# Key sums of a linear-attention layer with the exponentials as weights and the values moving, and variance from centred squares, in a four-layer kernel

## The chip, the cores and the metric

The kernel runs on one core of a Trainium2 chip. The metric is the device time of one execution in microseconds, lower is better; a kernel's time is the median of several runs. The core has a matrix engine (TensorE, PE in the profile, with its weight loads in a row of their own, PEld), a vector engine (VectorE, DVE), a scalar engine for functions and copies (ScalarE, ACT), GpSimd (POOL) and a queue that issues transfers (SyncE, SP). Each engine works through its own list of instructions in order and waits on semaphores for the others. Matmuls write to PSUM, eight banks of 512 float32 values in each of 128 partitions; the operands of matmuls lie in SBUF.

## The reference

Two kinds of layer alternate, A, B, A, B, each on a normalised input and added to it. There are 2048 tokens, 512 features, 32 heads of 16.

```python
def _A_ref(x, wqkv, w_phi, wo):
    B, S, D = x.shape
    H = 32; Dh = D // H
    qkv = (lambda x, *d: x.transpose(*d))((x @ wqkv).reshape(B, S, 3, H, Dh), 2, 0, 3, 1, 4)
    q, k, v = qkv[0], qkv[1], qkv[2]
    pq = jnp.einsum("bhsd,hdf->bhsf", q, w_phi)
    pk = jnp.einsum("bhsd,hdf->bhsf", k, w_phi)
    phi_q = jnp.concatenate([_softmax(pq, axis=-1), _softmax(-pq, axis=-1)], axis=-1)
    phi_k = jnp.concatenate([_softmax(pk, axis=-1), _softmax(-pk, axis=-1)], axis=-1)
    kv = jnp.einsum("bhsf,bhsd->bhfd", phi_k, v)
    z  = jnp.einsum("bhsf->bhf", phi_k)
    num = jnp.einsum("bhqf,bhfd->bhqd", phi_q, kv)
    den = jnp.einsum("bhqf,bhf->bhq", phi_q, z)[..., None] + 1e-6
    o = num / den
    return (lambda x, *d: x.transpose(*d))(o, 0, 2, 1, 3).reshape(B, S, D) @ wo
...
x = x + _A_ref(_layernorm(x, axis=-1), A_wqkv, A_w_phi, A_wo)
x = x + _B_ref(_layernorm(x, axis=-1), B_wqkv, B_wo)
x = x + _A_ref(_layernorm(x, axis=-1), A_wqkv, A_w_phi, A_wo)
x = x + _B_ref(_layernorm(x, axis=-1), B_wqkv, B_wo)
```

Layer A is linear attention: `kv` and `z` sum over all tokens, once per head, before any query can be answered. These are the key sums. Layer B is attention over eight earlier tokens at a distance of two, with the same weights in both of its layers.

## The kernel before

The 2048 tokens are 16 tiles of 128, held as four blocks b of four tiles; `x` stays in SBUF in bf16. Weights stay in SBUF too; at the start, w_phi is multiplied into the query and key columns of layer A's weights (`s_fold`), so that a projection gives `pq` and `pk` directly. L is 0 or 1, the first or second pair of layers.

Layer A runs in these steps. `s_a1`, per block: for each tile `mk` projects the keys (four matmuls, line 632), `ek` takes the exponentials of plus and minus the result (line 638, the index s is the sign), `mv` projects the values (line 644) and `ev` copies them into the tile `va`; VectorE adds up the 16 exponentials of each head and sign, ScalarE forms the inverse (`rr`), and VectorE multiplies it in (`mul`, line 690). `kv` (lines 697 to 709) then adds the tile to the key sums in PSUM. `va` holds 16 groups of 32 value columns (two heads) and a column of ones each. The 33 columns of a group are the weights of a matmul and 2 x 32 columns of exponentials move, so a tile takes 16 matmuls; two groups lie side by side in the halves of the array (`tile_position`). One bank holds all sums, with values on partitions and exponentials on columns. A matmul by zeros (line 700) prepares it.

`s_a2` projects the queries (line 737), takes their exponentials Eq (line 745) and their sums per head, S (line 753). `s_akv`, once per layer, turns the key sums into what the queries need: the bank is copied to `kvT`, four transposes put the exponentials on partitions (line 783), `z` writes the sums of ones, masked by head, into ZM (line 792), and `r` writes the value sums, masked by `mask2`, into R (line 796).

`s_a3`, per block: the denominator from ZM and Eq (line 821); `dr`, `ln` and `rho` go from VectorE to ScalarE and back to VectorE (lines 829 to 840); rho is spread over the features by matmuls (line 847, from where it goes to the products on line 855, in some cases through a copy `bs`) or, for two blocks of each layer, through a transfer. `s_a4`: the product of Eq and R (line 940), copied to `oT`, and the output projection in `s_out` (line 553).

`s_out` ends all layers. `res` adds the old x to the projection and sums each row (`sums`), on VectorE (line 571), or on ScalarE (line 568) after a matmul by the identity on PE (line 556). `sq` has ScalarE square the row and sum it (line 578). `var` (lines 588 and 590, VectorE) takes the squared mean off, and `s_norm` forms the inverse deviation (lines 450 and 453), the shift (line 457) and the normalised tile xn (line 466 or 468), which is transposed by PE (line 482) or by a transfer.

Layer B has its projections (line 967), elementwise products with eight shifted key windows (line 1059), sums per head by a matmul (line 1066), softmax, products with shifted values (line 1121), sums (line 1128) and `s_out`. The last block but the end of the second B layer goes another way, by small matmuls (lines 1185 to 1380).

What sets the order: each step is put into a thread named after its stage and engine, and `_ORDER` is a list of thread numbers in base 36; the program takes the next step of the thread that each number names. So it fixes every engine's list. `_CHOICE` has a digit for each step that either engine can do, 1 for VectorE (and, in `res`, for the identity matmul on PE with ScalarE), 0 for ScalarE, as `flex` and `copy` show; in `res` a 1 stands for the matmul. `_SLOTS` names the buffer or PSUM bank of each tile in turn. At the end a flag decides whether a general version is run instead (lines 1568 on); with these inputs it is not.

Of the kernel before, what the change touches and what calls it, by code (L numbers as in the profile page):

```python
# [16 lines left out]
P = 128  # L17
# [16 lines left out]
VCH = NB * 8 * DV  # L34
EST = (1, 3)
# [25 lines left out]
8 2 i 2e 3s e3 ce 2p 23 i a 5l i i 9 i i i 5o i i i i 4e e7 1m i 0 3u 3r 0 f i e c j b 2 k 3 4 j o 5q 1m l 3 m  # L61
p 1n 0 i 1 n 1t e4 o 1o q 1m 1p r 0 1m 1u s 1m z 5k z z 5 1m 1r 7 6 z 20 20 7 1q 1s 1t 21 21 t 20 20 1v 22 10
z 22 1t 7 1t 20 1w 22 t 11 24 24 13 u 12 16 12 1t t 15 1t v 12 12 22 x 18 14 1x d w w 1y 2c y 18 18 26 18 2d
1f 2d 2c 1z 2d 24 2d 27 17 19 18 1a 1b 21 1c 1d 22 21 22 39 1e 20 20 22 39 25 2c 3b 3a 3a 1f 3a 2d 3a 2f 2c 1f
1f 39 ch 22 2f 2d 2g 1g 29 1f 2d 1j 2f 2d 7 1h 29 1i 1k 3a 29 2n 29 2i 2n 3c 2o 2o 2o 2k 2o 2k 2q 1l cd 2h 2n
2a 2k 2f 2n 2k 3a 2o 2j 24 2q 2r 2q 2o 2o 2o 29 2y 28 2y 2y 3c 2l 2z 2v 2z 2s 2z 2z 2k 2y 2z 39 36 31 2z 36 2z
3a 3b 36 36 2v 31 2v 37 2v 31 2t 36 2z 36 2b 2b 2b 2b 2m 2m ci 36 36 2m 3a 2w 2m 2v 33 34 32 31 3c 35 2q 3c 36
3b 2x g 2x 2u 2x 30 37 2x 36 38 38 38 38 3i 3c 3h 3c 39 3b 3a 3j 3k 3k 3k 3c 3d 3c 3e 3l 3b 3m 3d 3e 5h 3n 3m
3c 3e 3e 3l 5i 3m 3q 3m 3m 4f 3m 3d 3l 5j 3e 3e 3m 5i 3m 3m 3v 3d 3e 3e bd 5h 5m 5n 5i 5i 5i 3m 3d 3e 7c 5h 7d
5p 5i 5i 5i 5r 3f 3g 3g 5i 3f 3g 5i 3w 3f 3z 3x 3f 3g 5s 3y 7e 40 41 3g 7d 5u 5v 7f 5t 3g 3p 41 42 41 41 44 3g  # L70
43 3g 43 5w 5x 5x 7f 45 46 43 43 47 43 7f 5y 3f 90 47 48 49 3g 4c 91 5x 41 4b 41 41 41 4a 92 5x 4d 60 91 4l 5z
61 5z 93 5z 4q 62 5z 4g 7d 4g 4g 4m 4q 63 ck 5z 7d 4r 93 4i 4l 63 66 64 67 7g 4s 7j 65 7h 7i 4h 4j 7k bo 4n 4q
4q 4u 4w 91 7l 4t 7l 7l 7m 7l 7o 68 7n 7n 4l 7p 3h 7n 7q 4w 93 4v 7n 4v 3o 91 4f 6a 7r 4o 6b 7n 6k 6f 69 4g 4k
4l 7r 6l 7s h 4w 6g 6k 6m 4p 6a 6c 6p 7t 7u 6a 6k 6f 6n 7v 4w 6k 6h 94 6r 6d 4x 4x b2 6r 4x 97 6o 98 4x 95 6f
69 7x 96 99 99 9a 4y 6i 99 7w 9b 6q 9c 6q 9d 9b 9b 99 9e 9b 6r 6a 6e 6f 6j 83 84 d4 6q 7y 9f 7y 9b 6r 6s 6s 6s
6s 9f 9h 9i 4y 9g 4w 8d 80 9j 7z 6t 6t 3t 88 6s 83 89 6t 88 88 88 8a 8b 8f 8c 7y 6r 7x 4x 9l 6u 9k 6u 4y 6u 4w
6q 6u 83 85 83 86 87 81 9r 9w 7y 9w 9s 9x 4v 82 4v 9w 6v 9y 9z 4z a1 6v 4z 6v 6w 4z 8e 6v 4z 6y 9m 6x 6z 70 9n
70 70 71 72 73 70 9m 74 72 72 8e 9m 50 50 50 75 50 9o 72 51 9r 52 76 53 8f 54 55 72 9p 9w 76 8f 79 55 77 7a 9r
9t 55 58 78 7b 9u 55 9r 56 9m 8f 59 8g 57 5a 57 8e 8g a3 8g 8g 57 bz b0 8e 9q 57 9v a0 5b 57 8h a3 5b bz 8h a3
8g 5d c0 5e 5c 5f c0 c0 b0 c0 bz 8h b1 5g b3 b1 8f b0 b1 b3 a2 b1 a4 c0 b1 a4 b1 a3 a4 a2 a4 b4 b5 a5 bz a5 8i  # L80
8i c0 8i a2 b3 a4 a2 c0 bx b6 c0 b3 a5 by bx by by b0 b7 bx by by by a3 8i bx 8j 8j b1 8j 8l a6 8k 8j 8m b1 8n
ap by aq aq ap a6 aq aq 8o 8o 8p by 8r 8o 8o 8q 8s 8q as 8t 8q as ap 8q au as ap a6 8u 8q a7 aq at 8u 8w aq bz
# [2043 lines left out]
```

## Time and profile before

| | |
|---|---|
| runs shown | 319.6, 319.8 and 320.18 us, median 319.8 |
| span of the profiled execution | 318.1 us |
| granted TensorE clock | 1.000 |
| instructions | 8900 |
| key sums (line 707) | 512 matmuls, from 44.4 to 203.7 us, in two bursts |
| squares (line 578) | 48 of 0.631 us on ScalarE |
| variance (lines 588 and 590) | 12 and 12 of 0.16 us on VectorE |
| transfers | 36.37 MB, mean 114 GB/s |

The span goes from the first to the last instruction of one execution, taken by the hardware profiler; it is 1.7 us under the median of the runs. Busy time counts an engine's instructions and not its waits; a matmul's row also holds the modelled time until its result is there, so the starts of neighbouring matmuls tell their real distance. The chain of waits is followed back from the last instruction, at each step to what released it or to the instruction before it on its engine.

### The profile page before, as it was taken

To read this page: it belongs to the slowest core of one execution; us is meant where nothing else is said; L and a number is where in the kernel's file an instruction comes from. 1 tells how busy PE (TensorE), PEld (TensorE's weight loads), DVE (VectorE), ACT (ScalarE), POOL (GpSimd) and SP (SyncE) were. 2 spreads that over 40 slices of the span, in tenths; PEclk is the share of its full clock that TensorE was granted. 3 is DMA by queue.
4 is the path that set the end of the run, shared out by engine and by line. 5 is a ranking of instruction groups with operands and counts; after the bars stand their busy time and mean duration, and the time that the engine had idled before them with its cause. 6 is when DMAs were issued, how large, how long until landed. Compare 5 with 4: busy or idle time off the path is not lost.

```text
span 318.1 us, 8900 instructions
## 1 busy us (share of the span) xinstructions
PE 307.7 (97%) x3578; PEld 152.9 (48%) x3578; DVE 295.6 (93%) x459; ACT 275.0 (86%) x639; POOL 47.2 (15%) x60
## 2 busy tenths in 40 slices
PE   8999999899999999999999999989999999999994
PEld 4644456445454444444444455544444544444552
DVE  6999996998999999999999999689998999999994
ACT  4999999999898778999999999899999867697751
POOL 6000000000004212000000000033141644045000
PEclk9999999999999999999999999999999999999999
DMA  7977100005794989939894600004289875565664
GB/s 203 358 186 148 36 2 4 2 19 145 165 178 100 156 141 136 144 66 140 145 134 62 69 0 2 4 19 134 59 185 137 140 133 134 105 178 126 158 152 170
DMA packets 45789, 36.37 MB, mean 114 GB/s; under 512 B 30832, under 2 KB 41136, under 8 KB 45744
## 3 DMA queue, kind: packets, MB, share of 16 engines
q1 hardware_dynamic: 45216, 35.75, 56.3%
q8 instruction: 29, 0.48, 0.7%
q14 instruction: 16, 0.13, 0.2%
q10 hardware_dynamic: 528, 0.02, 0.1%
HBM read 11.13 MB, written 3.25 MB: 45 GB/s over the span
## 4 chain that ended last, share of the span: by engine, by line
PE 87%; DVE 5%; ACT 5%; DMA 1%; issue 1%; SPq 0%; DVEq 0%; ACTq 0%
PE PS L967 23%; PE PS L553 18%; PE PS L632 9%; PE PS L644 9%; PE PS L737 6%; PE PS L1128 4%; PE PS L1066 4%; PE PS L1185 2%; DVE Eq L855 2%; PE PS L707 2%; PE PS L940 1%; PE PS L482 1%; PE PS L556 1%; PE PS L1200 1%; PE PS L1082 1%; DMA x<-in_A_x_dram 1%
## 5 line engine op out<-in xcount | busy, mean ns | idle before, releaser
L967 PE MATMUL PS<-xnT,WB 128*128 128x512 bf16 x336 | 76.8, 380 | 0.1
L1059 DVE TENSOR_TENSOR prod<-QT,K 128x4096 bf16<-128x4096 bf16 x28 | 63.4, 2287 | 0.5 <-POOL K L993 0.5
L1121 DVE TENSOR_TENSOR pav<-PT,Vg 128x4096 bf16<-128x4096 bf16 (+1 forms) x29 | 62.9, 2214 | 0.2
L967 PEld LDWEIGHTS <-WB 128*128 128x128 bf16 x336 | 37.3, 114 | 36.4 <-issue 3.3
L745 ACT ACTIVATE Eq<-PS 128x512 bf16<-128x512 f32 x64 | 36.3, 619 | 0.0
L638 ACT ACTIVATE Ek<-PS 128x512 bf16<-128x512 f32 x64 | 35.1, 622 | 0.2 <-PE PS L632 0.2
L553 PEld LDWEIGHTS <-oT 128*128 128x128 bf16 x236 | 21.9, 98 | 26.6 <-issue 1.3
L737 PE MATMUL PS<-xnT,WA 128*128 128x512 bf16 x128 | 32.0, 380 | 0.5 <-DVE s L829 0.3
L578 ACT ACTIVATE sqd<-x 128x512 bf16<-128x512 bf16 x48 | 29.9, 631 | 2.2 <-DVE x L571 2.0
L644 PE MATMUL PS<-WA,xnT 128*128 128x512 bf16 x128 | 31.6, 379 | 0.0
L632 PE MATMUL PS<-WA,xnT 128*128 128x512 bf16 x128 | 31.0, 379 | 0.2 <-ACT WA L204 0.2
L571 DVE SCALAR_TENSOR_TENSOR x<-PS,x 128x512 bf16<-128x512 f32 x46 | 30.2, 684 | 0.7 <-PE PS L553 0.7
L204 ACT CAST oT<-PS 128x512 bf16<-128x512 f32 (+1 forms) x50 | 26.7, 597 | 3.8 <-PE PS L1128 2.1
L553 PE MATMUL PS<-WoA,oT 128*128 128x512 bf16 x128 | 29.8, 380 | 0.0
L553 PE MATMUL PS<-WoB,oT 128*128 128x512 bf16 x108 | 26.5, 379 | 0.0
L204 ACT CAST K<-PS 128x512 bf16<-128x512 f32 x30 | 17.3, 593 | 3.1 <-PE PS L967 1.9
L632 PEld LDWEIGHTS <-xnT 128*128 128x128 bf16 x128 | 12.3, 98 | 15.2 <-issue 1.0
L644 PEld LDWEIGHTS <-xnT 128*128 128x128 bf16 x128 | 12.2, 98 | 14.5 <-issue 0.4
L690 DVE TENSOR_TENSOR Ek<-Ek,rk 128x4096 bf16<-128x4096 bf16 (+1 forms) x10 | 18.6, 1860 | 0.4 <-ACT rk L685 0.4
L737 PEld LDWEIGHTS <-WA 128*128 128x128 bf16 x128 | 11.6, 98 | 14.6 <-issue 1.7
L466 DVE TENSOR_SCALAR xn<-x,rstd,nmr 128x512 bf16<-128x512 bf16 x48 | 18.1, 424 | 0.6
L204 ACT CAST V<-PS 128x512 bf16<-128x512 f32 x26 | 15.2, 596 | 2.6 <-PE PS L967 2.6
(175 smaller groups left out, 505.1 us busy)
## 6 DMA issues: line engine op xcount, KB each, us to landing
Vg<-V SPq DMA_DIRECT2D x112, 131.5 KB, 4.3
Prho<-rd SPq DMA_DIRECT2D x8, 512.0 KB, 6.1
x<-in_A_x_dram SPq DMA_DIRECT2D x3, 512.0 KB, 6.6
WB<-in_B_wqkv_dram SPq DMA_DIRECT2D x3, 512.0 KB, 9.8
out_dram<-x SPq DMA_DIRECT2D x6, 256.0 KB, 2.3
wraw<-in_A_wqkv_dram SPq DMA_DIRECT2D x4, 256.0 KB, 4.5
vd<-Vs SPq DMA_DIRECT2D x2, 272.0 KB, 2.9
x<-in_A_x_dram SPq DMA_DIRECT2D x4, 128.0 KB, 3.4
```

The source lines that it names most:

```text
L204: self.nc.scalar.copy(out=out, in_=in_)
L553: nc.tensor.matmul(y[:], lhsT=lh(t, c), rhs=Wo()[:, c, :], start=(c == 0), stop=(c == NB - 1 and not onpe))
L571: nc.vector.scalar_tensor_tensor(out=xb[:, t, :], in0=T[t][:], scalar=1.0, in1=xb[:, t, :], op0=ALU.mult, op1=ALU.add, **kw)
L578: nc.scalar.activation(out=sqd[:], in_=xb[:, t, :], func=ACT.Square, accum_out=T["ss"][:, t:t + 1])
L632: nc.tensor.matmul(pk[:], lhsT=xnT[:, t, k, :], rhs=self.WA[:, k, D:2 * D], start=(k == 0), stop=(k == NB - 1))
L638: nc.scalar.activation(out=T["E"][:, t, s, :], in_=T["k", t][:], func=ACT.Exp, scale=1.0 - 2.0 * s)
L644: nc.tensor.matmul(pv[:], lhsT=xnT[:, t, k, :], rhs=self.WA[:, k, 2 * D:3 * D], start=(k == 0), stop=(k == NB - 1))
L737: nc.tensor.matmul(pq[:], lhsT=self.WA[:, k, hb * P:(hb + 1) * P], rhs=xnT[:, :, k, :], start=(k == 0), stop=(k == NB - 1))
L745: nc.scalar.activation(out=self.Eq[L, b][s][:, :, hb, :], in_=T[hb][:].rearrange("p (t i) -> p t i", t=4), func=ACT.Exp, scale=1.0 - 2.0 * s)
L967: nc.tensor.matmul(pp[:], lhsT=self.WB[:, k, i * D + c:(i + 1) * D:NB], rhs=xnT[:, :, k, :], start=(k == 0), stop=(k == NB - 1))
L1059: nc.vector.tensor_tensor(out=pr[:], in0=QT[:, c:c + 1, :].to_broadcast([P, NW, TB]), in1=win, op=ALU.mult)
L1121: nc.vector.tensor_tensor(out=pv, in0=PT[:, :, lo:lo + n].unsqueeze(1).to_broadcast([P, NB, 2, n]), in1=vw, op=ALU.mult)
```

## The change

The key sums are formed the other way round. `ek` writes the exponentials as eight groups of four heads, each with both signs side by side, 128 columns; `va` holds eight groups of 64 value columns and one column of ones. Per tile there are eight matmuls with the 128 columns of exponentials as weights and the 65 columns of `va` moving. The result has exponentials on partitions, so there are no transposes; it fills two banks, groups of even number in one and of odd number in the other, four pieces of 65 columns in each. In `s_akv`, four copies of 64 partitions bring the pieces into R, one per bank and sign; ZM is one product of R's ones column and the head mask; the value sums are masked by `mask4` where they lie in R. The zeroing matmul goes.

The square becomes that of the centred row: ScalarE squares sum - 512 x, with the row's sum as a bias of its own for each partition, so the sum of squares is 512 cubed times the variance, and `var` goes. PHI moves from a constant buffer to a slot that is used again.

`_ORDER`, `_CHOICE` and `_SLOTS` are new throughout. Over the whole program the choices have 14 identity matmuls in place of 17 among the full residuals, and VectorE has more of the copies.

```diff
@@ def sq(t) and norm, in s_out
-            nc.scalar.activation(out=sqd[:], in_=xb[:, t, :], func=ACT.Square, accum_out=T["ss"][:, t:t + 1])
+            nc.scalar.activation(out=sqd[:], in_=xb[:, t, :], func=ACT.Square, scale=-float(D),
+                                 bias=T["sums"][:, t:t + 1], accum_out=T["ss"][:, t:t + 1])
...
-        def var(lo, n):
-            if "q" not in T:
-                T["q"] = self.sm([4], "q")
-            u = T["sums"][:, lo:lo + n]
-            nc.vector.scalar_tensor_tensor(out=T["q"][:, lo:lo + n], in0=u, scalar=-1.0 / D, in1=u,
-                                           op0=ALU.mult, op1=ALU.mult)
-            nc.vector.tensor_tensor(out=T["q"][:, lo:lo + n], in0=T["q"][:, lo:lo + n],
-                                    in1=T["ss"][:, lo:lo + n], op=ALU.add)
-
         def norm(lo, n):
-            add(st, "DVE", var, lo, n)
-            V = {"var": lambda: T["q"][:, lo:lo + n], "sum": lambda: T["sums"][:, lo:lo + n]}
-            self.s_norm(st, key, b, V, tuple(range(lo, lo + n)), 1.0 / D, 1.0 / D)
+            V = {"var": lambda: T["ss"][:, lo:lo + n], "sum": lambda: T["sums"][:, lo:lo + n]}
+            self.s_norm(st, key, b, V, tuple(range(lo, lo + n)), 1.0 / D, 1.0 / D ** 3)
@@ s_a1
-                T["E"] = self.big([4, 2, D], "Ek")
-            nc.scalar.activation(out=T["E"][:, t, s, :], in_=T["k", t][:], func=ACT.Exp, scale=1.0 - 2.0 * s)
+                T["E"] = self.big([4, 8, 2, HQ], "Ek")
+            nc.scalar.activation(out=T["E"][:, t, :, s, :], in_=T["k", t][:].rearrange("p (g c) -> p g c", c=HQ),
+                                 func=ACT.Exp, scale=1.0 - 2.0 * s)
...
-                T["va"] = self.med([4, DH, H + 1], "vaug")
+                T["va"] = self.med([4, 8, HQ + 2], "vaug")
...
         def kv(t):
             if L not in self.kvp:
-                self.kvp[L] = self.ps()
-            K = self.kvp[L]
-            if b == 0 and t == 0:
-                nc.tensor.matmul(K[:], lhsT=self.kvT[:, 0:P], rhs=self.kvT[:], start=True, stop=True)
-            for r in range(4):
-                for h2 in range(2):
-                    for c in range(2):
-                        q = (2 * c + h2) * 4 + r
-                        a = K[64 * c:64 * c + H + 1, h2 * 256 + r * H:h2 * 256 + r * H + 1]
-                        out = bass.AP(a.tensor, a.offset, [list(a.ap[0]), [P, 2], [1, H]])
-                        nc.tensor.matmul(out, lhsT=T["va"][:, t, q, :], rhs=T["E"][:, t, :, q * H:(q + 1) * H],
-                                         start=(b == 0 and t == 0 and r == 0 and h2 == 0),
-                                         stop=(b == 3 and t == 3), tile_position=(0, 64 * c), skip_group_check=True)
+                self.kvp[L] = [self.ps() for _ in range(2)]
+            for g in range(8):
+                c = g // 2 * KVC
+                nc.tensor.matmul(self.kvp[L][g % 2][:, c:c + KVC], lhsT=T["E"][:, t, g, :, :],
+                                 rhs=T["va"][:, t, g, 0:KVC], start=(b == 0 and t == 0 and g < 2),
+                                 stop=(b == 3 and t == 3), skip_group_check=True)
@@ s_akv
-        def ev(dve):
-            self.copy(dve, self.kvT[:], self.kvp[L][:])
-
-
-        def tr():
-            T["t"] = pt = self.ps(BF16)
-            for g in range(4):
-                nc.tensor.transpose(pt[:, g * P:(g + 1) * P], self.kvT[:, g * P:(g + 1) * P], self.ident[:])
...
+        def sh(half, s, dve):
+            self.copy(dve, R[HQ * half:HQ * half + HQ, s, :, 0:KVC],
+                      self.kvp[L][half][HQ * s:HQ * s + HQ, 0:NB * KVC].rearrange("p (b c) -> p b c", c=KVC))
+
+        def z():
+            o = zm[:, 0:1]
+            dst = bass.AP(o.tensor, o.offset, [list(o.ap[0]), [NB * H, 2], [H + 8, NB], [1, 8]])
             m = self.maskH[:]
...
+            nc.vector.tensor_tensor(out=dst, in0=R[:, :, :, HQ:KVC].to_broadcast([P, 2, NB, 8]), in1=msk, op=ALU.mult)
 
         def r():
...
+            v = R[:, :, :, 0:HQ].rearrange("p s b (j d) -> p (s b) j d", d=DH)
+            nc.vector.tensor_tensor(out=v, in0=v, op=ALU.mult,
+                                    in1=self.mask4[:].unsqueeze(1).unsqueeze(3).to_broadcast([P, 8, 4, DH]))
...
+        for half in range(2):
+            for s in range(2):
+                self.flex(st, sh, half, s)
+        add(st, "DVE", z)
+        add(st, "DVE", r)
```

How the new order stands on VectorE at the handover of the key sums of the second layer A, before (PS is PSUM, `ZM_123` is ZM of that layer, `s` and Ds lead to rho):

```order
L690 TENSOR_TENSOR Ek<-Ek,rk 128x2048
L1402 TENSOR_TENSOR nb<-okc,sgn 128x2
L792 TENSOR_TENSOR ZM_123<-PS,maskH 128x2x2x8 x2
L796 TENSOR_TENSOR R<-PS,mask_98 128x256
L829 TENSOR_TENSOR s_3461<-PS,rS 128x256
L832 TENSOR_TENSOR Ds<-s_3461 128x128
L1410 TENSOR_TENSOR nok<-PS,thr 128x2
L1411 TENSOR_REDUCE nf<-nok 128x1
L840 TENSOR_TENSOR rho<-rS,Ds 128x256
```

and VectorE in the same place of the changed kernel, from the last product with the inverse sums on:

```order
L684 TENSOR_TENSOR Ek<-Ek,rk 128x2048
L204 CAST R<-PS 64x4x65
L771 TENSOR_TENSOR ZM_122<-R,maskH 128x2x4x8
L807 TENSOR_TENSOR s_3220<-PS,rS 128x256
L810 TENSOR_TENSOR Ds<-s_3220 128x128
L775 TENSOR_TENSOR R<-R,mask_98 128x8x64
L818 TENSOR_TENSOR rho<-rS,Ds 128x256
```

One of the four copies stands directly ahead of ZM, and the masking of R has moved behind the first steps towards rho; the other three copies are a row `CAST R<-PS 64x4x65 x3` on ScalarE, where one copy of `kvT` stood.

ScalarE at the first norm of the second layer B, before (`x_83` is block 0 of x, lnv and rstd give the inverse deviation):

```order
L568 ACTIVATE x_83,sums<-PS 128x512
L578 ACTIVATE sqd,ss<-x_83 128x512 x2
L835 ACTIVATE Ds<-Ds,deneps_t 128x128
L836 ACTIVATE Ds<-Ds 128x128
L204 CAST oT<-PS 128x512 x2
L578 ACTIVATE sqd,ss<-x_84 128x512
L450 ACTIVATE lnv<-q,eps_t 128x4
L453 ACTIVATE rstd<-lnv 128x4
```

and ScalarE at that norm in the changed kernel:

```order
L570 ACTIVATE x_83,sums<-PS 128x512
L580 ACTIVATE sqd,ss<-x_83,sums 128x512
L813 ACTIVATE Ds<-Ds,deneps_t 128x128
L814 ACTIVATE Ds<-Ds 128x128
L206 CAST oT<-PS 128x512 x2
L580 ACTIVATE sqd,ss<-x_83,sums 128x512
L452 ACTIVATE lnv<-ss,eps_t 128x4
L455 ACTIVATE rstd<-lnv 128x4
```

The logarithm now reads `ss` from ScalarE's own square in place of `q` from VectorE, the last square of the block stands right ahead of it, and each square reads `sums`.

153 lines of the change are left out of this document (70 added, 83 removed).

## The prediction

> **What bounds the kernel now.** I read first the page's busy times and the chain of waits, then busy time by stretches, then single groups and the timeline where the change acts.
>
> ```profile
> PE 307.7 (97%) x3578; PEld 152.9 (48%) x3578; DVE 295.6 (93%) x459; ACT 275.0 (86%) x639; POOL 47.2 (15%) x60
> PE 87%; DVE 5%; ACT 5%; DMA 1%; issue 1%; SPq 0%; DVEq 0%; ACTq 0%
> ```
>
> The first row is busy time by engine, the second the chain that ended last. TensorE carries 87% of that chain. But a busy PE row includes the modelled ends of matmuls, so I look where it is really full, in eight stretches (length, then PE, PEld, DVE, ACT, POOL busy, clock, DMA share, GB/s):
>
> ```profile
> 0.00:50.00 50.00, 48.34 (x456) 25.24 (x457) 45.74 (x102) 44.13 (x94) 5.54 (x30) 1.00 0.55 148
> 50.00:70.00 20.00, 18.45 (x452) 9.92 (x445) 15.94 (x36) 19.46 (x43) 0.47 (x2) 1.00 0.03 7
> 70.00:130.00 60.00, 59.99 (x476) 29.34 (x475) 58.44 (x87) 50.93 (x120) 8.93 (x12) 1.00 0.80 143
> 130.00:180.00 50.00, 50.00 (x407) 22.44 (x406) 49.65 (x53) 49.30 (x121) 0.39 (x1) 1.00 0.80 112
> 180.00:200.00 20.00, 19.97 (x229) 10.35 (x229) 19.09 (x33) 19.07 (x46) 0.00 (x0) 1.00 0.01 3
> 200.00:220.00 20.00, 17.47 (x479) 9.76 (x482) 16.20 (x41) 18.04 (x42) 5.26 (x2) 1.00 0.23 62
> 220.00:280.00 60.00, 60.00 (x449) 28.69 (x438) 56.82 (x78) 49.79 (x119) 19.31 (x12) 1.00 0.65 122
> 280.00:318.10 38.10, 33.47 (x673) 17.19 (x671) 33.68 (x36) 24.31 (x63) 7.27 (x2) 1.00 0.61 157
> ```
>
> From 70 to 200 and from 220 to 280 PE never rests: a matmul taken away there ends the kernel earlier. It rests where the key sums are handed over, 1.6 us in 50 to 70 and 2.5 us in 200 to 220, and in the tail. VectorE is close behind everywhere (58.4 of 60, 49.7 of 50), and from 130 to 180 ScalarE too (49.3 of 50). So a saving on PE counts, but only as far as DVE and ACT take no more.
>
> **Key sums.** Before, 512 short matmuls; a piece of the chain holds a quarter of them. The nearest thing to the new ones is line 1193: weights of 128 columns, 64 columns moving.
>
> ```profile
> 44.51 1.98 PE PS L707 x128
> L707 PEld LDWEIGHTS <-vaug 128*33 128x33 bf16 x512 | 7.9, 98 | 2.1 <-issue 1.7 <-ACT vaug L204 0.4
> 261.18 0.63 PE L1193 MATMUL PS<-xnT,WB 128*128 128x64 bf16 x16
> 261.64 0.59 PE L1200 MATMUL PS<-WB,xnT 128*128 128x512 bf16 x2
> L1193 PEld LDWEIGHTS <-WB 128*128 128x128 bf16 x16 | 0.6, 98 | 0.2
> 187.20 0.89 PE PS L482 x16
> ```
>
> 128 in 1.98 us are 15.5 ns each (two run side by side in halves of the array), 512 make 7.9 us. The 16 of line 1193 start at 261.18 and the next group at 261.64: 28.8 ns each. One load reads 98 ns with 33 columns and with 128, so wider weights show no price. 256 new ones (65 columns) by 28.8 make 7.4 us: -0.5. Upper bound: line 482, whose 16 with 128 moving columns take 55.6 ns each; 256 x 55.6 = 14.2 us, +6.3. Lower bound: nothing below the moving columns of the old pairs, 31 ns a pair, so no further gain. I take 28.8, the same shape but for one column.
>
> The Trainium skill, TensorE: Matmul & The Clock Gate, section LDWEIGHTS (loading the stationary operand), speaks against the change: a load is said to take its column count divided by 1.2, in ns, so 107 ns at 128 columns, and 256 of them would be an estimated 27 us in place of 7.9. By that rule the time would be an estimated 338 us; line 1193 in this trace, at 28.8 ns with 128 columns, does not agree.
>
> **Other TensorE work.** The eight transposes, the two zeroing matmuls and, by the new choices, three of 17 residual matmuls go.
>
> ```profile
> 204.59 0.40 PE L783 MATMUL PS<-ident,kvT 128*128 128x128 bf16 x4 [0.68 <-ACT kvT L204]
> 204.83 0.17 PE L1406 MATMUL PS<-nb,ones 128*128 128x2 bf16 x1
> 204.99 0.56 PE PS L753 x32
> L700 PE MATMUL PS<-kvT 128*128 128x512 bf16 x2 | 0.8, 379 | 0.0
> L556 PE MATMUL PS<-x,ident 128*128 128x512 bf16 x17 | 6.4, 379 | 0.0
> 23.57 0.86 PE PS L737 x4
> 10.88 1.73 PE PS L632 x7
> ```
>
> Four transposes take 0.24 us, so eight 0.5. Four full matmuls take 0.86 in the chain, 0.216 each: two and three of them are 0.43 and 0.65. With the key sums PE does 2.0 us less, spread over stretches in which it is full.
>
> **The handover.** At 204.59 PE had waited 0.68 us for the copy of the sums. In its place come four copies of 64x260, and the product for ZM waits for all four. In layer 0 all are VectorE's; in layer 1 ScalarE does three in a row and VectorE one. At 0.38 us (ACT, 128x256 below) three are about 1.1 us, ZM 0.2 more. Behind the last key sum PE now has four projections and 32 sums of exponentials, some 0.86 + 0.56 us (the rows of 23.57 and 204.99), ahead of the matmuls that read ZM; before it had almost nothing. So the wait nearly goes: I take -0.6, bounds -0.7 and +1.0 (all four copies in a row and no cover). What is late next is rho, as now: it still follows VectorE, ScalarE, VectorE.
>
> **ScalarE.** Every Square now has a bias per partition.
>
> ```profile
> L578 ACT ACTIVATE sqd<-x 128x512 bf16<-128x512 bf16 x48 | 29.9, 631 | 2.2 <-DVE x L571 2.0
> L835 ACT ACTIVATE Ds<-Ds,deneps_t 128x128 f32<-128x128 f32 x8 | 3.3, 413 | 1.1 <-DVE Ds L832 1.0
> L836 ACT ACTIVATE Ds<-Ds 128x128 f32<-128x128 f32 x8 | 2.5, 309 | 0.2
> L204 ACT CAST oT<-PS 128x512 bf16<-128x512 f32 x48 | 26.1, 606 | 2.1 <-PE PS L940 0.9 <-DVE prod L1059 0.6 <-PE PS L1128 0.4
> L204 ACT CAST kvT<-PS 128x256 bf16<-128x256 f32 x1 | 0.4, 378 | 0.0
> L204 ACT COPY xnT<-PS 128x1024 bf16<-128x1024 bf16 x3 | 3.0, 1009 | 0.3 <-PE PS L482 0.3
> L468 ACT ACTIVATE xn<-x,nmr,rstd 128x512 bf16<-128x512 bf16 x16 | 12.9, 818 | 0.2 <-DVE nmr L457 0.2
> L568 ACT ACTIVATE x<-PS 128x512 bf16<-128x512 f32 x17 | 10.0, 593 | 4.0 <-PE PS L556 3.8
> L886 ACT CAST bs<-PS 128x512 bf16<-128x512 f32 x14 | 7.6, 587 | 0.1
> ```
>
> Two operations on one tile, with and without a bias tensor, differ by 0.104 us; 48 Squares pay 4.8-5.0. The new choices take 12 copies away (-7.2), three residuals (-1.8), and bring three copies of the sums (+1.1), four of 1024 less one half (+3.5), two normalisations (+1.6) and two bs (+1.2): -1.6. ACT carries about 3.3 more. Two thirds of the Squares stand where ACT has room (50.9 of 60, 49.8 of 60); 16 belong to the layer-1 norms around 130 to 180, where it has 0.7 us: 1.6 us there. I let half through: +0.8, bounds 0 and +4.8.
>
> **VectorE.** The 24 variance operations go; it takes over casts.
>
> ```profile
> L590 DVE TENSOR_TENSOR q<-q,ss 128x4 f32<-128x4 f32 x12 | 2.0, 168 | 2.5 <-ACT sqd L578 1.5
> L588 DVE SCALAR_TENSOR_TENSOR q<-sums 128x4 f32<-128x4 f32 x12 | 1.9, 162 | 0.1
> ACT lnv L450 <- DVE q L590: 1.2, 4, 0.5
> L202 DVE CAST vaug<-PS 128x512 bf16<-128x512 f32 x7 | 4.8, 688 | 0.1
> L571 DVE SCALAR_TENSOR_TENSOR x<-PS,x 128x512 bf16<-128x512 f32 x46 | 30.2, 684 | 0.7 <-PE PS L553 0.7
> L829 DVE TENSOR_TENSOR s<-PS,rS 128x256 f32<-128x256 f32 x8 | 3.4, 420 | 1.6 <-ACT Eq L745 0.8 <-PE PS L821 0.5 <-ACT rS L760 0.3
> L202 DVE COPY xnT<-PS 128x1024 bf16<-128x1024 bf16 x6 | 4.0, 682 | 1.0 <-PE PS L482 0.6 <-ACT Ek L638 0.3
> L466 DVE TENSOR_SCALAR xn<-x,rstd,nmr 128x512 bf16<-128x512 bf16 x48 | 18.1, 424 | 0.6
> ```
>
> -3.9 for lines 588 and 590; ten more casts +6.9; three residuals +2.1; five quarter copies of the sums at 0.42, +2.1; four copies of 1024 fewer, one of 512 more -2.3; two normalisations fewer -0.8; masks and the products with bs -0.9. Net +3.2. Of it I let +0.5 through, because the variance steps stood in a waiting chain (ScalarE waited 1.2 us for line 590, four times) and this wait goes; bounds -1.2 and +3.2.
>
> **At nothing.** The sums now hold two PSUM banks; PE shows no rest in 180 to 200, where one was held, so six others should do. If not, each lacking bank costs an eviction of 0.6 us; two bound it, 0 to +1.2. The start is reordered (six idle matmuls instead of eleven ahead of the first transposes); the copies and folds before the first key projection are as many: 0, bounds -0.7 and +0.7.
>
> **Sum**, on the profiled execution: 318.1 - 2.0 - 0.6 + 0.8 + 0.5 = 316.8. It ends 1.7 under the median of the runs, 319.8, so the median should be **318.5 us**, chance 0.48, its own range 317.0 to 319.4.
>
> **Rivals.** (1) The new order also closes rests: half of the 4.1 us that PE rests in 50 to 70 and 200 to 220, with nothing back from DVE and ACT: 318.1 - 2.0 - 2.1 = 314.0, median 315.7. For it: the four projections put behind the last sum. Against: rho's chain over three engines is unchanged. 0.15. (2) No change: DVE and ACT give back just what PE saves, 319.8. It asks for 2.6 of their added 6.5; 0.08. (3) Slower: VectorE becomes the bound. Place: 70 to 180, where it has 1.9 us of room in 110, and the tail; price: its whole net 3.2 and the 1.6 of ScalarE's Squares there, less 2.6: +2.2, 322.0. It decides once more than 2.6 of these 4.8 come through. For it: the two rows with 58.4 of 60 and 49.7 of 50. Against: most of the added casts replace ScalarE's, so a bank comes free as early. 0.23. (4) Slower: the weights of 128 columns do not hide behind 65 moving ones, and a pair takes 55.6 ns: 6.9 us more than the sum, 323.7, median 325.4; it decides above 34 ns. At a load's whole 98 ns each it would be 17.7 more, median 336. Against both stands line 1193. 0.06, of it 0.01 for the 98 ns. The second is the mechanism of the Trainium skill's rule above, and by that rule, too, the trace disagrees.
>
> **Numbers.** A measurement of this kernel tells 0.2%, 0.64 us, from no change. Faster: 0.43 of the forecast's 0.48 and all of (1), 0.58. Same: the other 0.05 and (2), 0.13. Slower: (3) and (4), 0.29. The range, 315.3 to 322.4, reaches to (1) and (3) and leaves out (4) and the ends of both, some 0.2.
>
> **What would show it.** Key sums at 28 to 30 ns each in the timeline; Square near 735 ns; no wait above 0.3 us ahead of the first matmuls on ZM; PE's rest in the stretches from 70 to 200 still under 0.3 us. The prediction is wrong if the new matmuls take over 34 ns, if PE rests for VectorE's casts by more than 2 us in 70 to 200, or if the first key projections begin more than 1 us later than the row of 10.88 has them.

## The result: slower by 5 to 6 us, and the profile after

The changed kernel is slower. In a first series its median was 324.98 us (324.33 to 328.56, 6 runs) beside 319.70 for the kernel before: ratio 1.0174, 95% interval 1.0152 to 1.0197. In a second series it was 325.90 (324.82 to 328.08) beside 320.01: 1.0197 (1.0164 to 1.0229). The forecast was 318.5, and its range ended at 322.4.

The first profiled execution was the slowest of all its six (328.56); the last section returns to it. The profile read here is that of an ordinary execution of the same kernel, 325.89 us, span 324.1, 6.0 more than before. The page has as busy times and chain of waits:

```profile
PE 308.1 (95%) x3309; PEld 152.9 (47%) x3309; DVE 298.3 (92%) x448; ACT 277.1 (86%) x632; POOL 40.3 (12%) x60
PE 60%; ACT 15%; DVE 8%; DMA 8%; SPq 5%; issue 2%; ACTq 0%; DVEq 0%
```

TensorE is busy for 308.1 us, before for 307.7, in a span that is 6 us longer: it does no more than before and rests 5.6 us more. Its part of the chain fell from 87% to 60%; ScalarE, transfers and SyncE's queue came in. The same stretches as in the prediction, with the same columns (length, then PE, PEld, DVE, ACT, POOL busy, clock, DMA share, GB/s):

```profile
0.00:50.00 50.00, 46.96 (x334) 24.73 (x335) 43.82 (x100) 44.36 (x92) 5.96 (x32) 1.00 0.49 138
50.00:70.00 20.00, 18.55 (x430) 10.31 (x427) 17.65 (x38) 19.21 (x42) 0.24 (x1) 1.00 0.01 3
70.00:130.00 60.00, 59.45 (x472) 29.07 (x471) 57.08 (x82) 50.91 (x116) 7.92 (x10) 1.00 0.83 149
130.00:180.00 50.00, 49.84 (x374) 21.82 (x373) 49.23 (x45) 49.71 (x119) 4.66 (x4) 1.00 0.62 106
180.00:200.00 20.00, 19.83 (x168) 10.16 (x166) 19.35 (x34) 19.40 (x45) 0.00 (x0) 1.00 0.12 28
200.00:220.00 20.00, 17.39 (x385) 10.09 (x383) 16.62 (x36) 18.57 (x43) 4.02 (x3) 1.00 0.17 43
220.00:280.00 60.00, 59.46 (x478) 28.09 (x477) 57.68 (x80) 49.67 (x117) 13.80 (x9) 1.00 0.74 131
280.00:324.10 44.10, 36.63 (x685) 18.60 (x683) 36.84 (x39) 25.29 (x65) 3.69 (x2) 0.98 0.53 132
```

The rest of TensorE is length less busy time. It grew by 1.4 us in the first 50, by 0.8 from 70 to 200, by 0.5 from 220 to 280 and by 2.8 behind 280 (7.47 against 4.63). Most of the loss lies behind the second handover of the key sums, for which the forecast had no term of its own.

To compare the loads there, both kernels have to be cut at the same step and not at the same time: at 200 us the changed kernel is already some 2 us late, so work that stood ahead of 200 before stands behind it now. The cut taken here is the start of the first matmul that reads ZM in the second layer A, 205.38 us before and 207.63 after. From there to the end, before and after:

```profile
205.38:330.00 124.62, 106.24 (x1424) 52.30 (x1410) 103.65 (x145) 87.71 (x212) 31.83 (x15) 1.00 0.53 117
```

```profile
207.63:330.00 122.37, 106.02 (x1408) 51.85 (x1404) 105.29 (x142) 86.37 (x207) 21.52 (x13) 0.99 0.58 119
```

The rows end behind the spans, 318.1 and 324.1. So of the 6.0 us, 2.2 arise ahead of this cut and 3.8 behind it, and of TensorE's 5.6 us of added rest 4.0 lie behind it. VectorE, in all 2.7 us busier, has 1.1 more ahead of the cut and 1.6 more behind it (105.29 against 103.65). What it does behind it is seen by groups (busy us and mean ns behind the bar), VectorE alone, before:

```profile
L571 DVE SCALAR_TENSOR_TENSOR x<-PS,x 128x512 bf16<-128x512 f32 x21 | 13.9, 684 | 0.5 <-PE PS L553 0.5
L202 DVE CAST oT<-PS 128x512 bf16<-128x512 f32 x7 | 4.7, 686 | 0.0
L202 DVE CAST V<-PS 128x512 bf16<-128x512 f32 x2 | 1.3, 675 | 0.0
L202 DVE CAST K<-PS 128x512 bf16<-128x512 f32 x1 | 0.7, 685 | 0.0
```

and after:

```profile
L573 DVE SCALAR_TENSOR_TENSOR x<-PS,x 128x512 bf16<-128x512 f32 x23 | 14.8, 683 | 0.0
L204 DVE CAST oT<-PS 128x512 bf16<-128x512 f32 x9 | 5.9, 684 | 0.0
L204 DVE CAST K<-PS 128x512 bf16<-128x512 f32 x2 | 1.4, 682 | 0.0
L204 DVE CAST Qs<-PS 128x512 bf16<-128x512 f32 x1 | 0.7, 686 | 0.0
L204 DVE CAST V<-PS 128x512 bf16<-128x512 f32 x1 | 0.7, 685 | 0.0
L204 DVE CAST QT<-PS 128x512 bf16<-128x512 f32 x1 | 0.7, 683 | 0.0
```

Two more residuals, two more copies of oT, one more each of K, Qs and QT, one fewer of V: six operations of 0.68 us net, 4.1 us that the new choices add. Against them stand the eight variance steps that are gone here (-1.4), two products of Eq that read PSUM in the kernel before and `bs` now (-0.7) and shorter normalisations (-0.6), and small differences. Last, the two operations whose price the forecast took from neighbours, the first two rows by groups, the others from the timeline (start, us):

```profile
L694 PE MATMUL PS<-vaug,Ek 128*128 128x65 bf16 x256 | 10.1, 193 | 0.1
L580 ACT ACTIVATE sqd<-x,sums 128x512 bf16<-128x512 bf16 x48 | 34.8, 744 | 1.5 <-DVE x L573 1.2
```

```profile
49.12 1.18 PE L694 MATMUL PS<-vaug,Ek 128*128 128x65 bf16 x32
50.14 1.02 PE L724 MATMUL PS<-xnT,WA 128*128 128x512 bf16 x4
```

32 key sums from 49.12 to 50.14 are 31.9 ns each; a Square takes 744 ns.

### The profile page after: what moved, and what is told of

Same layout as the page of the kernel before. It is cut to its first block, busy times and chain, and to the rows that moved or that the text cites. A ratio compares the mean times of both kernels' runs of the same rounds, so it can differ in the third digit from the quotient of the medians.

```text
span 326.8 us, 8364 instructions
## 1 busy us (share of the span) xinstructions
PE 312.2 (96%) x3309; PEld 154.3 (47%) x3309; DVE 299.1 (92%) x448; ACT 277.2 (85%) x632; POOL 38.5 (12%) x60
## 4 chain that ended last, share of the span: by engine, by line
PE 59%; ACT 11%; DMA 9%; DVE 8%; issue 8%; SPq 4%; POOL 1%; ACTq 0%; DVEq 0%; POOLq 0%
PE PS L945 14%; PE PS L555 11%; PE PS L724 5%; PE PS L625 5%; PE PS L638 5%; DMA Vg<-V 3%; PE PS L1044 3%; DMA xnT<-xn 2%; PE PS L694 2%; ACT sqd L580 2%; DMA Prho<-rd 2%; DVE pav L1099 2%; DVE Ek L684 2%; PE PS L1163 2%; SPq L1006 2%
## 5 line engine op out<-in xcount | busy, mean ns | idle before, releaser
L945 PE MATMUL PS<-xnT,WB 128*128 128x512 bf16 x336 | 78.7, 386 | 0.3 <-ACT QT L206 0.3
L580 ACT ACTIVATE sqd<-x,sums 128x512 bf16<-128x512 bf16 x48 | 34.8, 744 | 1.3 <-DVE x L573 1.0
L631 ACT ACTIVATE Ek<-PS 128x512 bf16<-128x512 f32 x64 | 35.8, 634 | 0.1
L573 DVE SCALAR_TENSOR_TENSOR x<-PS,x 128x512 bf16<-128x512 f32 x49 | 32.1, 685 | 1.6 <-PE PS L555 1.5
L638 PE MATMUL PS<-WA,xnT 128*128 128x512 bf16 x128 | 32.1, 379 | 0.0
L724 PE MATMUL PS<-xnT,WA 128*128 128x512 bf16 x128 | 31.9, 379 | 0.0
L625 PE MATMUL PS<-WA,xnT 128*128 128x512 bf16 x128 | 31.2, 379 | 0.2 <-ACT Ek L631 0.2
L555 PE MATMUL PS<-WoA,oT 128*128 128x512 bf16 x128 | 31.1, 390 | 0.0
L206 ACT CAST oT<-PS 128x512 bf16<-128x512 f32 (+1 forms) x48 | 26.0, 599 | 1.7 <-PE PS L1106 1.1
L206 ACT CAST K<-PS 128x512 bf16<-128x512 f32 x27 | 15.7, 602 | 7.2 <-PE PS L945 7.0
L206 ACT CAST QT<-PS 128x512 bf16<-128x512 f32 x25 | 14.4, 595 | 4.5 <-PE PS L945 4.5
```

The costliest lines, as they stand in the source:

```text
L206: self.nc.scalar.copy(out=out, in_=in_)
L555: nc.tensor.matmul(y[:], lhsT=lh(t, c), rhs=Wo()[:, c, :], start=(c == 0), stop=(c == NB - 1 and not onpe))
L573: nc.vector.scalar_tensor_tensor(out=xb[:, t, :], in0=T[t][:], scalar=1.0, in1=xb[:, t, :], op0=ALU.mult, op1=ALU.add, **kw)
L580: nc.scalar.activation(out=sqd[:], in_=xb[:, t, :], func=ACT.Square, scale=-float(D), bias=T["sums"][:, t:t + 1], accum_out=T["ss"][:, t:t ...
L625: nc.tensor.matmul(pk[:], lhsT=xnT[:, t, k, :], rhs=self.WA[:, k, D:2 * D], start=(k == 0), stop=(k == NB - 1))
L631: nc.scalar.activation(out=T["E"][:, t, :, s, :], in_=T["k", t][:].rearrange("p (g c) -> p g c", c=HQ), func=ACT.Exp, scale=1.0 - 2.0 * s)
```

## The experiments

In all of them "old" is the order, the choices and the buffers of the kernel before with the changed arithmetic, and "new" those of the changed kernel; times are medians, and each ratio is to the kernel before in the same series. **To ZM** is the start of the first matmul that reads ZM in the second layer A, and **behind ZM** the span less that, both of the one profiled execution: before 205.4 and 112.7, after 207.6 and 116.5.

**The changed kernel again, unchanged.** The profile above is of this run.

> The changed kernel as it is, profiled again, because its first profiled execution (span 326.8 us) lies at the top of its six times and its granted clock falls to 0.83 near 290. Whatever the theory, the median should be 324.3 to 325.5 us and the span below 325.5. The idle time of TensorE that every execution has should come back: about 1.5 to 2 us more than before by the first key projection, about 2 us by 200, about 2 us around the handover of layer 1 (205 to 220). If the waits for the transposed tiles near 255 and for the query tile near 289 are gone, they belonged to that one execution.

1.0197 (1.0164 to 1.0229); its interval overlaps that of the first series, and the median, 325.90, lies a little above the 325.5 expected. The wait for the query tile near 289 was there again, 1.56 us at 286.92.

**Parts of the arithmetic alone, in the old order.**

```diff
 old_order_squares
-  func=ACT.Square
+  func=ACT.Square, scale=-float(D), bias=T["sums"][:, t:t + 1]
 def var(lo, n)
-  nc.vector.scalar_tensor_tensor(...); nc.vector.tensor_tensor(...)
+  pass
-  self.s_norm(st, key, b, V, tuple(range(lo, lo + n)), 1.0 / D, 1.0 / D)
+  self.s_norm(st, key, b, V, tuple(range(lo, lo + n)), 1.0 / D, 1.0 / D ** 3)
 old_order_keysums: ek, va, kv, ZM and R of the change; the step of the one copy now makes four
-  self.copy(dve, self.kvT[:], self.kvp[L][:])
+  for i, d in enumerate("DADA"): sh(i // 2, i % 2, d == "D")
 old_order_both: the two together
```

> The kernel before with the centred squares alone: its order stays, the two VectorE instructions of the variance (11 times) are gone and ScalarE's 48 squares take 0.11 us more each, 5.3 us in all. Theory 'order' (the loss comes from where the new order puts work, not from the arithmetic): 319.2 to 321.0. Rival 'bias' (ScalarE is so close to binding from 130 on that most of 5.3 us reaches the end): 322 to 325. Rival 'key sums': as 'order', since no key sum is touched.

> The kernel before with the new key sums alone, in its own order: exponentials of four heads as weights, two PSUM banks instead of one held over the key sums (7 of 435 other tiles move to another bank for that), no transposes; the four copies at the handover stand where the one copy stood, two on VectorE and two on ScalarE. The buffer of zeros is 256 columns wide and read twice, so that the wider handover tile fits. Theory 'order': 318 to 320.5. Rival 'key sums' (pairs of 32 ns, the second bank and the handover's longer VectorE work cost the time): 322 to 325. Rival 'bias': as 'order'.

> All of the arithmetic of the changed kernel in the order of the kernel before: both edits of the two kernels above together. Theory 'order': 318 to 321, so 4 us or more below the changed kernel. If either rival is right, 323 to 326, as the changed kernel. A time in between would split the loss: what is above 319.7 belongs to the arithmetic in this order, the rest to the new order.

The squares: 320.61, 1.0017 (1.0007 to 1.0026). The key sums: 323.69, 1.0112 (1.0095 to 1.0128); both: 324.71, 1.0144 (1.0123 to 1.0165). This looked as if the key sums themselves cost 3.5 us. The timeline of old_order_keysums at the first handover says otherwise (start, us, and in brackets the wait and who ended it):

```profile
51.78 0.83 ACT L206 CAST R<-PS 64x260 bf16<-64x260 f32 x2 [2.46 <-DVE R L204]
52.63 0.60 ACT L742 ACTIVATE Eq<-PS 128x512 bf16<-128x512 f32 x1
...
55.66 1.02 PE L734 MATMUL PS<-xnT,WA 128*128 128x512 bf16 x4 [2.81 <-ACT Eq L742]
```

My own placement had given two of the four copies to ScalarE. There they waited 2.46 us for the last key sums, the exponentials that need nothing of them stood behind in ScalarE's list, and TensorE waited 2.81 us for these. So:

```diff
 old_order_keysums_dve, old_order_both_dve
-  for i, d in enumerate("DADA"): sh(i // 2, i % 2, d == "D")
+  for i, d in enumerate("DDDD"): sh(i // 2, i % 2, d == "D")
```

> The new key sums alone in the order of the kernel before, as in old_order_keysums, but all four copies at the handover on VectorE (there: two on VectorE, two on ScalarE). In that run's trace ScalarE stood 2.46 us in front of its first copy, with exponentials of queries queued behind, and TensorE lost 2.99 us at 55.7 and 1.54 us at 208.7 for them. Theory 'queue' (a copy in ScalarE's line waits for the last key sums and holds the exponentials behind it; the pairs and the second bank cost nothing): both gaps go, 318.8 to 320.6. Rival 'second bank' (query projections find no free bank while two are held): the gaps stay whatever engine copies, 322.5 to 324.5. Rival 'pairs' (32 ns a pair): the loss is spread and stays, 322 to 324.

> All of the arithmetic of the changed kernel in the order of the kernel before, the four copies of each handover on VectorE. Theory 'queue' and 'order' together: the 3.5 us of the copies go and the squares' 0.6 us stay, 319.5 to 321.3, some 4 us or more below the changed kernel. Rival 'second bank': 323 to 325.

320.51, 1.0016 (1.0004 to 1.0028), and 320.62, 1.0020 (1.0008 to 1.0032). The loss was one of placement; the new key sums, second PSUM bank included, cost 0.5 us (0.1 to 0.9). The whole arithmetic in the old order costs 0.6 to 0.8 us and on balance saves nothing. It is seen at ZM, in old_order_both_dve:

```profile
206.24 0.63 PE L811 MATMUL PS<-Eq,ZM 128*32 128x128 bf16 x32 [1.44 <-DVE ZM L776]
```

where the kernel before waited 0.68 us for the copy. In the changed kernel this wait is gone:

```profile
207.63 1.08 PE L799 MATMUL PS<-Eq,ZM 128*32 128x128 bf16 x64
```

The other 4.4 to 5.3 us, then, are the new order's.

**Two places of the new order, mended one at a time.**

```diff
 new_order_start: four of the idle matmuls ("i" in _ORDER) stand ahead of the first transposes
-  0 4 b i 1m i 1m 9 3 i 3 30 0 j o 1 23 i i k
+  0 4 b i i i i i 1m i 1m 9 3 3 30 0 j o 1 23 k
 new_order_spq: on SyncE, three writes of value rows behind the transfers for Qbd
-  ds i8 ig gq ig i0 ... i1 ia ia ia ig ia ia ... gf ia ig
+  ds i8 gq i0 ... i1 ia ia ia ia ia ia ig ig ig ... gf ig
```

> The changed kernel with four idle matmuls moved ahead of its first transposes: ten stand there instead of six, none between the second transposes and the first folds. Theory 'cold start' (the first transposes and the idle matmuls behind the second run at half pace and hold the folds): the folds start 0.6 us sooner and the median falls by 0.4 to 1.0 us, to 324.3 to 325.5 beside a changed kernel at 325.3. Rival (ScalarE and the loads set the first 50 us, as the changed kernel's share of busy ScalarE there says, 44.4 of 50): within 0.3 us of the changed kernel.

> The changed kernel with three writes of value rows in SyncE's line moved behind the sixteen transfers of block-diagonal queries (the last nine of them stood behind those writes, which wait for values that ScalarE casts late). In the trace TensorE waited 1.6 to 1.7 us near 287 for the last of these transfers. Theory 'late SyncE' (the end is set by SyncE's line from 277 on): the last of the transfers is issued near 282 instead of 285, TensorE's wait goes, and the median falls by 1 to 2.5 us, to 322.8 to 324.3. Rival 'only moved' (the value rows' reads come later by as much, and the last window's gathers with them): within 0.7 us of the changed kernel, or slower.

325.43, 1.0151 (1.0125 to 1.0177): no gain; the folds now waited 1.22 us for a copy (wT) on VectorE. And 327.35, 1.0237 (1.0192 to 1.0282), no better and perhaps worse: the wait that it was made to remove, the only one over 1 us behind 220 in the changed kernel,

```profile
286.92 0.30 PE L1270 MATMUL PS<-Qbd,K 64*32 64x160 bf16 x9 [1.56 <-DMA Qbd<-Qs]
```

was gone, and in new_order_spq there stood

```profile
298.07 0.21 PE L1316 MATMUL PS<-Vx,et 128*32 128x68 bf16 x1 [2.53 <-DMA Vx<-vd]
```

From 270 to 300 SyncE issues one transfer after another, and here a transfer moved ahead made another late.

**Cutting the order in two.** Up to a certain step the threads are taken as in one order, behind it as in the other; the choices go with their steps.

```diff
 new_until_handover1: new up to the second handover (token 978 of 1482), old behind
-_ORDER, _CHOICE, _SLOTS
+new[:978] + the steps that are left, as old has them
 old_until_handover1: the converse;  old_until_handover0: old up to the first handover, new behind
 new_in_layer0: new up to the end of the first pair of layers, old behind
```

> The arithmetic of the changed kernel throughout. Its new order runs until the copies and masks of the second handover (near 207 us); all steps left then follow in the order of the kernel before (13 of 757 tiles lie in another buffer for that). The old order throughout took 320.6, the new one 325 to 326. Theory 'last window' (most of the loss arises behind the second handover, where the last window's transposed tiles come 6 us later than before and SyncE's line cannot catch up): 321.3 to 322.7. Rival 'spread' (it arises in the first 207 us: cold start, ScalarE full from 130 on): 323.5 to 325.5.

> The converse: the order of the kernel before until the same place, the new order behind it. Theory 'last window': 323 to 325. Rival 'spread': 320.5 to 322.

> The new order until the first key projections of layer 1 (near 125 us), the old one for what is left then. The idle time of TensorE says that the new order is 1.1 us behind at 130. Theory 'last window': 321 to 322. Rival 'spread': 322 to 324, and if the first layer alone is to blame, 324 and more.

> The old order until the first handover (near 53 us), the new one behind it: the start of the kernel before with the rest of the changed kernel. Theory 'last window': 324 to 325.5, less than 1 us below the changed kernel. Rival 'start' (what is lost before the handover is carried to the end and more): 321 to 323.5.

| | median | ratio (95%) | to ZM | behind ZM |
|---|---|---|---|---|
| old_order_both_dve | 320.62 | 1.0020 (1.0008 to 1.0032) | 206.2 | 113.1 |
| new_until_handover1 | 321.54 | 1.0049 (1.0032 to 1.0066) | 207.6 | 112.2 |
| old_until_handover1 | 326.03 | 1.0199 (1.0175 to 1.0222) | 209.0 | 114.3 |
| old_until_handover0 | 325.52 | 1.0182 (1.0160 to 1.0204) | 208.0 | 115.4 |
| new_in_layer0 | 331.10 | 1.0361 (1.0338 to 1.0383) | 215.9 | 113.0 |

With the new order ahead of the handover and the old one behind, only 0.9 us of these are left; with the new one behind it, the medians show the whole loss whatever stands ahead. By the spans the part behind ZM is smaller in these two, +1.2 and +2.3 on old_order_both_dve against +3.4 in the changed kernel. new_in_layer0 tells nothing of that: it loses 8 us ahead of ZM, at its own seam, where TensorE waits 3.6 us once for a residual. old_until_handover1 is not a clean converse either: its buffers differ, it reaches ZM 2.8 us late after a wait of 1.81 us for R at its seam, and it came out above the 323 to 325 expected.

**What is it behind the handover?** Behind ZM VectorE was busy for 103.65 us before, 102.70 in old_order_both_dve and 102.32 in new_until_handover1, but 105.29 after. The row of old_order_both_dve:

```profile
206.24:330.00 123.76, 105.43 (x1400) 52.23 (x1410) 102.70 (x137) 87.87 (x210) 32.55 (x15) 0.99 0.54 117
```

Ahead of ZM the same two kernels, which differ only in order, choices and buffers, have 193.04 and 192.98 us. So what the new choices put on VectorE, 2.6 us, stands wholly behind the handover. Two suspects: this load, and the late normalisation of the last A block of the second pair. In the changed kernel VectorE has

```profile
247.12 2.28 DVE L1037 TENSOR_TENSOR prod<-QT,K 128x4096 bf16<-128x4096 bf16 x1
...
249.40 2.28 DVE L1037 TENSOR_TENSOR prod<-QT,K 128x4096 bf16<-128x4096 bf16 x1
251.60 1.38 DVE L468 TENSOR_SCALAR xn<-x,rstd,nmr 128x512 bf16<-128x512 bf16 x4
```

two products ahead of the normalised tiles, whose transposes SyncE issues at 253.12 and 259.25, before both at 249.62.

```diff
 new_early_norm (VectorE's list; SyncE's two transposes side by side)
-  prod, prod, xn x4
+  xn x4, prod, prod
 new_old_engines: the 24 digits of _CHOICE behind the handover that differ, as old has them
 new_early_norm_engines: both
 old_late_norm: the same two products ahead of xn, in the old order
-  xn x4, prod, prod
+  prod, prod, xn x4
```

> The changed kernel with one thing moved: on VectorE the normalizations of the last two tiles of layer 1's first half stand ahead of the two products of 2.29 us that stood in front of them, and on SyncE the last transposes follow the ones before at once instead of four gathers later. Theory 'late normalization' (the last window's chain - transposes, queries, their block-diagonal copies, gathers - starts too late and the end follows it): the transposes leave by 251 and 255 instead of 253 and 259, and the median falls by 2 to 4 us, to 321.3 to 323.5 beside a changed kernel at 325.4. Rival 'engines' (three more residual additions and more copies on VectorE behind the handover): within 0.8 us of the changed kernel.

> The changed kernel's order with the choice of engine, for the copies, residuals and normalizations behind the second handover, of the kernel before (24 choices differ). Rival 'engines': 321.5 to 323.5. Theory 'late normalization': 324.5 to 326.5, since the two products still stand in front.

> Both of the two kernels above at once. If each is half of the cause: 321 to 322.5, below either. If the normalization is the cause alone: as new_early_norm within 0.7 us. If neither is: 324.5 and more.

> The converse in the old order with the changed kernel's arithmetic (320.6 us): the last tile's normalization put behind two products on VectorE, and on SyncE the transposes of the tile before it behind four gathers, as the new order has them. Theory 'late normalization': 322 to 324.5. Rival 'engines': 320.3 to 321.5.

new_early_norm: 325.16, 1.0148 (1.0128 to 1.0168), and the end came no earlier beyond the intervals. But the move did little: VectorE now waited 2.00 us for the inverse deviation from ScalarE, the normalised tiles started at 250.35 instead of 251.60, and the transposes left together at 254.97, still 5 us after those of before and not by 251 and 255 as expected. So it does not tell what the late norm costs. new_old_engines: 332.95, 1.0393 (1.0363 to 1.0423); with the early norm 334.58, 1.0434 (1.0403 to 1.0465). That answers nothing about the load: with other engines under the same order TensorE waited 4.3 us once for a residual on VectorE. Order and choices belong together. old_late_norm: 323.94, 1.0117 (1.0099 to 1.0135), behind ZM 114.5 against 113.1.

So, fewer digits: three copies of 0.68 us, one each of K, Qs and oT, which stand in the changed kernel between VectorE's products where it hardly rests (two of them in the stretch from 260 to 280, busy 19.34 of 20):

```profile
262.07 0.69 DVE L204 CAST Qs<-PS 128x512 bf16<-128x512 f32 x1
262.67 2.28 DVE L1037 TENSOR_TENSOR prod<-QT,K 128x4096 bf16<-128x4096 bf16 x1
...
278.10 0.68 DVE L204 CAST K<-PS 128x512 bf16<-128x512 f32 x1
278.70 4.48 DVE L1099 TENSOR_TENSOR pav<-PT,Vg 128x4096 bf16<-128x4096 bf16 x2
...
285.31 0.68 DVE L204 CAST oT<-PS 128x512 bf16<-128x512 f32 x1
```

```diff
 new_three_copies_act: digits 312, 335 and 369 of _CHOICE
-  1 1 1
+  0 0 0
 old_three_copies_dve: the converse, in the old order
-  0 0 0
+  1 1 1
```

> The changed kernel with three copies between 260 and 290 us (one each of queries of the last window, of keys and of attention output, 0.68 us each) given to ScalarE, which is busy 13 of 20 us there. Theory 'VectorE' (it is full from 240 on and sets the end): the median falls by 1.2 to 2.2 us, to 323.0 to 324.2. Rival 'transfers' (the last gathers and query copies set the end, VectorE waits for them): within 0.7 us of the changed kernel's 325.4.

> The converse in the old order with the changed kernel's arithmetic (320.6 us): the same three copies given to VectorE instead of ScalarE. Theory 'VectorE': 321.8 to 322.8. Rival 'transfers': 320.2 to 321.2.

new_three_copies_act: 323.50 (322.29 to 326.12), 1.0134 (1.0102 to 1.0165), 1.5 to 2.4 us under the two medians of the changed kernel (1.3 to 2.0 by the ratios), and inside what the theory of the load expected; its interval just overlaps with theirs. In its profile behind ZM 113.7, 2.8 less than after, and in the row from ZM on:

```profile
207.78:330.00 122.22, 105.19 (x1397) 52.20 (x1404) 103.33 (x139) 87.73 (x210) 22.02 (x13) 0.99 0.55 119
```

VectorE has 2.0 us less than the 105.29 above, the three copies of 0.68. Its busy time alone does not set the end, though: old_until_handover0 has 107.0 behind ZM (its ten normalisations there take 579 ns each, 406 in the changed kernel) and yet needs 1.1 us less from there. The converse cost far more than the move had given, 324.62, 1.0140 (1.0120 to 1.0161), +4.0 on old_order_both_dve. It is confounded: old_late_norm and old_three_copies_dve were built like old_until_handover1, wait 1.8 us for R at 207.5, ahead of the moved steps, and show a clock of 0.78 to 0.88 in 205 to 215. Of their +1.4 and +2.5 behind ZM, part is the clock, so neither converse proves its cause. No version was faster than the kernel before.

## Why the prediction was wrong

**Where the 6.0 us of the span come from**, by the profiles: the arithmetic +0.9 to ZM and +0.3 behind (old_order_both_dve against before); the new order +1.4 to ZM (207.6 against 206.2) and +3.4 behind it (116.5 against 113.1). In medians the arithmetic is 0.6 to 0.8 and the new order 4.4 to 5.3.

**The step that failed** is VectorE's: "Net +3.2. Of it I let +0.5 through". The net was right, +2.7 by the busy times. But I took it as one sum over the kernel and asked only how much of it comes through, not where it stands. The new choices' part of it, 2.6 us, stands wholly behind the second handover, where VectorE is busy for 105.29 of 116.5 us and little is left behind it to make up for a delay. There the new order costs 3.4 us, more than the upper bound of this term, +3.2 for the whole kernel; VectorE's added work is 2.6 of them and 0.8 is its own longer rest, an account of the time and not yet of the cause. For ScalarE I had asked where the work stands (two thirds where it has room); for VectorE I did not. Its rivals inherited this: rival (3) named the engine and the tail, but put the place at 70 to 180, where TensorE rests only 0.7 us more, and its price, +2.2, was again the net. That the load behind the handover costs time is borne out by new_three_copies_act, which gives 1.3 to 2.4 us of the 4.4 to 5.3 back, with six runs and an interval that just overlaps. How the rest divides among the residuals and the copies that were not moved, the transfers of Qbd and Vx, and the late norm is open, and so is what the new order loses ahead of ZM. Two savings that the forecast counted on failed as well, PE's and the handover's; they come next.

**PE, -2.0.** "I take 28.8" was 31.9: 256 make 8.2 us in place of 7.9, +0.3 and not -0.5. What differs from the row it was taken from is at least one column, two banks in turn and a sum that goes on over 16 tiles; which of them costs 3 ns was not tried. The weights of 128 columns do hide, at 31.9 ns a pair, and rival (4) is false; that its 325.4 meets the measured time is chance. The transposes, the zeroing and the residual matmuls did go, but TensorE is no less busy (+0.4 us in all), and what was taken away did not bring the end forward: in the old order with the new arithmetic 0.8 of the 0.9 us of transposes and zeroing came back as a longer wait at ZM, 1.44 in place of 0.68.

**The handover, -0.6.** Right at its place in the new order: no wait ahead of the first matmul on ZM. But rho and Eq came late next: TensorE's rest in 200 to 220 is 2.61 us, before 2.53, with waits of 0.68 for `bs`, 0.58 for Eq and 0.84 for rho. The step said that rho is late next "as now", and still took the gain; it should have been 0.

**ScalarE, +0.8.** 744 ns a Square against the 735 forecast, and net +2.1 against 3.3. The old order with the squares alone (and without the variance steps) costs 0.2 to 0.8 us by its interval: right, if a little high. The Trainium skill, ScalarE: Activation LUTs, section What ACT_TABLE_LOAD costs, says that each per-partition operand of an activation adds about 93 ns; the 113 measured here are near it and a fifth higher.

**At nothing.** The two banks: old_order_keysums_dve bounds them, with all else of the key sums, at 0.9 us. The start: the first key projections began at 11.12, before at 10.35 (the row of 10.88 has seven of them, and one stands ahead of it), 0.77 later and just past my bound of 0.7; the first 50 us hold 1.4 us more of rest, and new_order_start did not bring it back.

Of the signs named for the forecast two failed, if by little: the key sums at 28 to 30 ns (31.9), and a rest under 0.3 us from 70 to 200 (0.88). Of those named as proof against it (over 34 ns, over 2 us of rest in 70 to 200, a start 1 us late) none came true, and yet it was wrong: none of them looked behind the second handover.

## What to carry to other kernels

Where a change brings a new order and new choices, compare each engine's load stretch by stretch, not in total: what is added to an engine can stand wholly in the stretch that ends the kernel. Cut both kernels at the same step, not at the same time, or the later kernel seems to have moved work back. Measure new arithmetic in the old order, apart from the new order, and cut the order in two before looking for single waits. Give a copy that must wait to an engine that has nothing urgent behind it in its list.

## What the runs showed of the hardware

In these traces the granted clock fell behind some short waits, and not behind every one. In the first profiled execution of the changed kernel, stretches of 5 us with the columns as above:

```profile
215.00:220.00 5.00, 3.50 (x82) 1.59 (x68) 4.61 (x12) 4.37 (x10) 3.59 (x3) 0.82 0.56 136
220.00:225.00 5.00, 5.00 (x94) 2.13 (x93) 4.06 (x8) 3.83 (x11) 5.00 (x2) 0.83 0.41 103
...
290.00:295.00 5.00, 5.00 (x55) 1.94 (x47) 2.16 (x3) 3.44 (x9) 1.01 (x2) 0.67 0.56 149
```

and its timeline at the second place:

```profile
289.52 0.29 PE L1270 MATMUL PS<-Qbd,K 64*32 64x160 bf16 x9 [1.91 <-DMA Qbd<-Qs]
...
289.99 3.54 PE L945 MATMUL PS<-xnT,WB 128*128 128x512 bf16 x8
...
293.89 1.92 PE L945 MATMUL PS<-xnT,WB 128*128 128x512 bf16 x8
```

After one wait of 1.91 us eight matmuls take 3.54 us, the next eight of the same shape 1.92. If the slow part runs at half rate, 0.67 is 3.3 us of it (2 x 0.33 x 5), and 0.82 with 0.83 is 3.5 us (2 x 0.35 x 5): each time some 1.7 us of matmul work lost, which is worked out, not measured. Two of them are 3.4 us, and this execution was 3.6 over the median of its series. old_three_copies_dve has the same after a wait of 1.8 us (0.80 and 0.86, 3.4 us by the same sum), and so has old_late_norm (0.88 and 0.78), while old_until_handover1, with a wait of 1.81 at the same place, shows none; new_order_spq has it after its 2.53 us. So a wait of some 2 us may cost nearly as much again, by chance. Kernels with the new order behind the handover spread over 1.7 to 4.8 us between runs; old_order_squares, old_order_keysums_dve, old_order_both_dve and new_until_handover1 over 0.8 to 1.1. This fits, but was not tested, and two kernels speak against it: new_early_norm's slowest run, 327.58, shows a clock of 1.000, and old_late_norm, with the slow clock in its profile, spreads over 1.0 in its four runs.

The Trainium skill, TensorE: Matmul & The Clock Gate, section What's actually happening, gives half rate after at least one idle window of about 3.4 us, with windows that run freely. The slow stretches here agree with half rate for about one window; that they follow waits of 1.8 to 2.5 us, and at 215 no single wait over 0.85, does not agree with a window that is idle throughout.
